# A decay-weighted attention and a gated feed-forward on one core: later copies of turned keys, weight words through a byte conversion, weight guards moved into the loop, and a new list of work

## The chip, the core and the metric

The kernel runs on one core of a Trainium2 chip. Its engines work side by side, each on its own queue of instructions: TensorE (PE), VectorE (DVE), ScalarE (ACT) and GpSimd (POOL); SyncE (SP) starts most transfers. The metric is the device time of one execution in microseconds, the median of the runs shown.

## What is computed

For each of 4 batches and 8 heads a 48x48 state runs over 768 tokens. Its output, 3072 rows of 384, goes through a gated feed-forward of width 1536. The weights come as float64.

```python
for t in range(S):
    kt, vt, rt, wt = (k[:, :, t], v[:, :, t], r[:, :, t], w[:, :, t])
    cur = np.einsum('bhd,bhe->bhde', u[None] * kt, vt)
    y[:, :, t] = np.einsum('bhd,bhde->bhe', rt, state + cur)
    state = wt[:, :, :, None] * state + np.einsum('bhd,bhe->bhde', kt, vt)
...
gate = 1.0 / (1.0 + np.exp(-(x @ w_gate)))
val = x @ w_val
return (gate * val @ w_out).astype(np.float32)
```

## The kernel before

Attention is cut into 24 chunks q of 128 tokens: batch q % 4, position q // 4. Four chunks of one position make a tile n of 512 rows for the feed-forward, and there are six tiles. The feed-forward's width is cut into 12 blocks f of 128; a block's weights (a third each for gate, value and output) are 128 x 1152 values.

For a chunk, `load_pin` and `load_tok` fetch decay, keys and queries, and values. VectorE scans the decay (`scan_k`, `prep_r`) and scales keys and queries. The keys are turned: early by TensorE (`turn_k`, then `take_k` copies them from its bank to `kT`); from chunk 10 on (`AWAY`) by VectorE, block by block, and by two transfers through device memory, `far_k` out and four reads `bk` back, after which ScalarE's three copies in `take_k` (L428, L430) make `kT`. TensorE computes scores and sums, VectorE masks (`mask`), TensorE applies (`states`, `mix`), ScalarE takes the result out (`take_y`), and it is turned into columns (`turn_x`, `take_x`, `rest_x`). The term of the current token goes through GpSimd (`bonus1`, `bonus2`, `bonus4`) and VectorE (`bonus3`). For the chunks in `LANES` (0, 1, 2) GpSimd multiplies queries by keys once (`in_lanes`), and TensorE sums with small matmuls (L421).

A float64 weight becomes a float32 word by bits. `w_body` and `w_sign` put the high word, shifted left by 3 and with its top bits kept, into a spare tile `temp`; `w_tail` joins the top 3 bits of the low word and writes over the low word. That is three VectorE passes. `w_guard` squares the high words on ScalarE and sums two tests, of which `check_bounds` makes a flag; if it is set, the slow path `general` runs behind everything. For tile 0, the blocks in `EXACT` (0 to 4) are multiplied as float32, in parts of 1 or 2 chunks (`SINGLE`, halves); the others are split into a high and a low part (`w_hi` on ScalarE, `w_lo` on VectorE) and take three matmuls where one stood.

The first stage holds chunks 0 to 7, all weights and tile 0. Its order comes from a planner (`Plan`). Each operation has an engine, a cost, what it waits for and a rank; the ranks come from the lists `TURNS` and `COMES` (the order of transfers on SP) and from the offsets in `LAGS` and `LATE`. `keep_busy` matmuls fill TensorE early on.

The loop then runs tiles 1 to 5, 12 steps each, in an order written by hand. A step issues `gate` and `sigmoid`, `value`, `hidden`, `hidden_hi` and `hidden_lo`, and `down` of the step before. It has four slots (0 to 3) in which other work is queued by `at(time, ...)`, where time counts slots from the loop's start. The visit to chunk q (`both`: states and outputs of q, scores and sums of q + 1) stands at a time that is 7 modulo 12. What prepares chunk q + 1 stands up to eight slots before. `take_k` of a key that goes through memory stands at `late`, time - 3, ahead of a step's sigmoid on ScalarE. In the first loop tile the `EXACT` blocks are split (`WHEN`). `leave` copies a finished tile out, on ScalarE and, for the last tile, on VectorE too.

In the rows below L638 and L641 are a step's matmuls for gate (`pg`) and value (`pu`), L681 those of `down` (`po`), L635 and L677 the exact ones, L651 the sigmoid, L658 `hidden`, L662 `hidden_hi`, L722 the fillers, L280 and L281 the guards, L285, L288 and L291 the words, L300 and L303 the split, L333, L336 and L340 the bonus products, L347 `in_lanes`.

## Time and profile before

| what | value |
|---|---|
| median of 3 runs | 560.25 us (557.87 to 560.35) |
| the profiled execution's own time | 565.31 us |
| its span, first to last instruction | 563.5 us |
| TensorE busy | 541.9 us (96%) |
| VectorE busy | 339.4 us (60%) |
| ScalarE busy | 218.9 us (39%) |
| GpSimd busy | 105.4 us (19%) |
| moved by DMA | 63.80 MB, mean 113 GB/s |

The busy shares are means over a first stage and a loop with different limits, so the rows below go by stretches. Matmuls are pipelined: the durations of single groups overlap, and the starts of the groups tell the pace.

### The profile page before, as it was taken

To read this page: it belongs to the slowest core of one execution; us is meant where nothing else is said; L and a number is where in the kernel's file an instruction comes from. 1 tells how busy PE (TensorE), PEld (TensorE's weight loads), DVE (VectorE), ACT (ScalarE), POOL (GpSimd) and SP (SyncE) were. 2 spreads that over 40 slices of the span, in tenths; PEclk is the share of its full clock that TensorE was granted. 3 is DMA by queue.
4 is the path that set the end of the run, shared out by engine and by line. 5 is a ranking of instruction groups with operands and counts; after the bars stand their busy time and mean duration, and the time that the engine had idled before them with its cause. 6 is when DMAs were issued, how large, how long until landed. Compare 5 with 4: busy or idle time off the path is not lost.

```text
span 563.5 us, 12729 instructions
## 1 busy us (share of the span) xinstructions
PE 541.9 (96%) x5395; PEld 448.0 (80%) x5395; DVE 339.4 (60%) x503; ACT 218.9 (39%) x428; POOL 105.4 (19%) x86
## 2 busy tenths in 40 slices
PE   8889899999999999999999999999999999999994
PEld 6777788877878888878888878887888888888883
DVE  5678998899677765656655656665655632321221
ACT  4568743743544334334234334234334322312211
POOL 5241503061103203203203303203203200000000
PEclk9698999999999999999999999999999999999998
DMA  8379502811343343243343343333343310100001
GB/s 325 139 263 422 202 0 100 303 64 30 128 126 111 94 145 116 97 128 105 98 145 101 113 130 106 94 103 136 119 124 112 95 31 1 56 2 0 1 0 62
DMA packets 30292, 63.80 MB, mean 113 GB/s; under 512 B 9617, under 2 KB 18706, under 8 KB 28690
## 3 DMA queue, kind: packets, MB, share of 16 engines
q1 hardware_dynamic: 28066, 58.97, 30.3%
q10 hardware_dynamic: 2160, 3.93, 1.8%
q8 instruction: 44, 0.72, 0.5%
q14 instruction: 22, 0.18, 0.1%
HBM read 52.14 MB, written 10.75 MB: 112 GB/s over the span
## 4 chain that ended last, share of the span: by engine, by line
PE 69%; DVE 10%; DMA 8%; ACT 5%; issue 2%; POOL 2%; SPq 1%; ACTq 0%; DVEq 0%
PE po L681 17%; PE pg L638 13%; PE pu L638 13%; PE pu L641 6%; PE pg L641 6%; DMA pin<-dec 3%; DVE sg L658 2%; DMA bk<-far_k 2%; PE po L677 2%; PE pa L457 2%; DMA raw<-wts 2%; DVE w L303 2%; PE py L477 2%; PE py L471 2%; PE pa L463 1%
## 5 line engine op out<-in xcount | busy, mean ns | idle before, releaser
L658 DVE TENSOR_TENSOR sg<-pu,sg 128x512 f32<-128x512 f32 (+2 forms) x78 | 50.6, 648 | 124.9 <-PE pu L641 104.7
L681 PE MATMUL po<-hh,w 128*128 128x512 f32 x402 | 124.8, 392 | 0.0
L638 PE MATMUL pg<-x,w 128*128 128x512 f32 x402 | 105.0, 396 | 0.0
L638 PE MATMUL pu<-x,w 128*128 128x512 f32 x402 | 102.5, 390 | 0.0
L651 ACT ACTIVATE sg<-pg 128x512 f32<-128x512 f32 (+2 forms) x78 | 44.1, 565 | 117.3 <-PE pg L641 87.5
L333 POOL TENSOR_TENSOR bon<-tok,ub 128x384 f32<-128x384 f32 x21 | 38.3, 1822 | 273.2 <-DVE x L626 180.9
L662 ACT CAST hh<-sg 128x512 fp32r<-128x512 f32 x67 | 41.5, 620 | 120.6 <-DVE sg L658 120.6
L638 PEld LDWEIGHTS pu<-x,w 128*128 128x128 f32 x402 | 75.2, 188 | 15.6
L681 PEld LDWEIGHTS po<-hh,w 128*128 128x128 f32 x402 | 74.9, 188 | 15.2
L638 PEld LDWEIGHTS pg<-x,w 128*128 128x128 f32 x402 | 73.7, 188 | 15.7
L681 PE MATMUL po<-hl,w 128*128 128x512 f32 x201 | 78.3, 390 | 0.2 <-DVE hl L666 0.2
L666 DVE TENSOR_TENSOR hl<-sg,hh 128x512 fp32r<-128x512 f32 x67 | 47.6, 711 | 41.7 <-ACT hh L662 41.7
L641 PE MATMUL pg<-x,w 128*128 128x512 f32 x201 | 56.6, 390 | 0.0
L641 PE MATMUL pu<-x,w 128*128 128x512 f32 x201 | 56.5, 389 | 0.0
L681 PEld LDWEIGHTS po<-hl,w 128*128 128x128 f32 x201 | 37.7, 188 | 8.7 <-DVE hl L666 0.8
L641 PEld LDWEIGHTS pg<-x,w 128*128 128x128 f32 x201 | 37.7, 188 | 8.0
L641 PEld LDWEIGHTS pu<-x,w 128*128 128x128 f32 x201 | 37.7, 188 | 7.9
L354 POOL TENSOR_TENSOR at<-eye,a 128x512 f32<-128x512 f32 x24 | 30.1, 1255 | 63.8 <-DVE a L340 55.7
L361 DVE TENSOR_TENSOR_SCAN eg<-pin,ends 112x516 f32<-112x516 f32 x24 | 30.7, 1278 | 8.3 <-DMA pin<-dec 5.7
L547 DVE COPY_PREDICATED at<-after,pa 128x512 f32<-128x512 int32 x24 | 17.7, 736 | 22.6 <-PE pa L463 20.1
L336 POOL TENSOR_TENSOR bon<-bon,tok 128x384 f32<-128x384 f32 x21 | 29.2, 1392 | 1.6
L381 DVE TENSOR_TENSOR_SCAN eg<-pin,heads 112x516 f32<-112x516 f32 x24 | 29.4, 1226 | 0.0
(101 smaller groups left out, 681.9 us busy)
## 6 DMA issues: line engine op xcount, KB each, us to landing
pin<-dec SPq DMA_DIRECT2D x23, 772.0 KB, 5.1
raw<-wts SPq DMA_DIRECT2D x12, 1152.0 KB, 10.1
tok<-tok SPq DMA_DIRECT2D x21, 576.0 KB, 4.3
y<-o ACTq DMA_DIRECT2D x15, 256.0 KB, 2.5
far_k<-bk SPq DMA_DIRECT2D x14, 256.0 KB, 2.0
bk<-far_k SPq DMA_DIRECT2D x56, 64.0 KB, 2.0
far_x<-bx SPq DMA_DIRECT2D x12, 192.0 KB, 3.2
bon<-far_x SPq DMA_DIRECT2D x48, 48.0 KB, 2.0
```

Of the source, the lines that this page charges most:

```text
L333: nc.gpsimd.tensor_tensor(out=bon[q], in0=tk[q][:, 0:DM], in1=ub, op=ALU.mult)
L336: nc.gpsimd.tensor_tensor(out=bon[q], in0=bon[q], in1=tk[q][:, DM:2 * DM], op=ALU.mult)
L354: engine.tensor_tensor(out=att[q], in0=eye.unsqueeze(1).unsqueeze(1).broadcast_to(shape), in1=a0, op=ALU.mult)
L361: nc.vector.tensor_tensor_scan(out=e[:, 516:0:-1], data0=t[:, 516:0:-1], data1=ends[:, 516:0:-1], initial=0.0, op0=ALU.mult, op1=ALU.add,)
L381: nc.vector.tensor_tensor_scan(out=e[:, WW:WW + 516], data0=t[:, 0:516], data1=heads[:, 0:516], initial=0.0, op0=ALU.mult, op1=ALU.add,)
L638: nc.tensor.matmul(t, lhsT=w[f][:, cols], rhs=x[n][:, a, k, spot], start=k == 0 and j == 0, stop=False)
L641: nc.tensor.matmul(t, lhsT=whi[f][:, cols], rhs=x[n][:, 1, k, i0 * C:i1 * C], start=False, stop=k == NKT - 1)
L651: nc.scalar.activation(sg, hid["g", n, f, i0], AF.Sigmoid)
L658: nc.vector.tensor_tensor(out=sg, in0=hid["u", n, f, i0], in1=sg, op=ALU.mult)
L662: nc.scalar.copy(hh, hid["s", n, f, i0])
L666: nc.vector.tensor_tensor(out=hl, in0=hid["s", n, f, i0], in1=hid["hi", n, f, i0].bitcast(F32), op=ALU.subtract)
L681: nc.tensor.matmul(to, lhsT=w[f][:, cols], rhs=h, start=first and i == 0, stop=last and i == 2, skip_group_check=True)
```

## The change

- `take_k` of keys that go through memory moves from `late` (time - 3) to time - 1.
- `w_body` and `temp` go. ScalarE reads the top byte of each low word, scales it by 1/32 and writes its integer part, the top 3 bits, over the low word (`top_bits`). VectorE joins the shifted high word (`w_sign`) and restores the top bits (`w_tail`), both in place.
- `w_guard` leaves the first stage. In the loop, from its second tile on and once in 12 slots, a block's float64 weights are fetched again into a buffer that is free by then (`again`), and three ScalarE passes test them (`w_square`, `w_small`, `w_large`). A small probe of the conversion's rounding joins the flag.
- The list: four exact blocks in place of five, three of them starting in quarters (`SINGLE`); no `LANES`; block 11 in two parts (`PAIRS`); new `TURNS`, `COMES`, `LAGS`, `LATE`; fillers stop once `po` exists.
- In the last tile the last part of `leave` is split in two, over ScalarE and VectorE and over two issuing engines.

```diff
-TURNS = "c0 w0 c1 c2 c3 w1 w2 w3 w4 w5 c4 w6 c5 w7 c6 w8 w9 w10 w11 c7"
-COMES = "ub p0 w0 p1 t0 w1 w2 t1 p2 t2 t3 w3 p3 w4 w5 w6 w7 t4 p4 w8 p5 t5 w9 p6 t6 p7 w10 w11 p8 t7 t8 t9 p9"
-SINGLE = [0]
-WIDE = [5, 6, 7, 8, 9, 10, 11]
-EXACT = [0, 1, 2, 3, 4]
+TURNS = "c0 w0 c1 c2 w1 c3 w2 w3 c4 c5 w4 w5 w6 w7 w8 c6 w9 w10 c7 w11"
+COMES = "ub p0 w0 t0 p1 w1 t1 t2 p2 w2 w3 p3 t3 t4 w4 t5 w5 p4 w6 p5 w7 p6 t6 w8 w9 w10 p7 t7 p8 t8 w11 p9 t9"
+SINGLE = [0, 1, 3]
+WIDE = [4, 5, 6, 7, 8, 9, 10, 11]
+EXACT = [0, 1, 2, 3]
...
-LAGS = [0, 11.5, -11.5, 103.0]
-LATE = dict(b3=-1.2, wl=-15.0, xl=17.5, wg=6.5, gd=51.5)
+LAGS = [0, -37.0, -28.5, 86.5]
+LATE = dict(b3=0.15, wl=1.0, xl=30.5, gd=72.5, wb=-2.0)
...
-PAIRS = []
-LANES = [0, 1, 2]
-RK = "POOL"
+PAIRS = [11]
+LANES = []
+RK = "DVE"
...
-    def w_guard(f):
-        sq = stage.tile([P, 3 * DM], BF16, tag="sq", name=f"sq{f}")
-        nc.scalar.activation(sq, word(f, 1, F32), AF.Square, accum_out=acc_s[:, f:f + 1])
-        nc.scalar.activation(sq, sq, AF.Relu, bias=1.0, scale=-1.0 / TINY ** 2, accum_out=acc_t[:, f:f + 1])
-
     def w_body(f):
-        t = temp[f] = stage.tile([P, 3 * DM], I32, tag="temp", name=f"temp{f}")
-        nc.vector.tensor_scalar(out=t, in0=word(f, 1), scalar1=3, scalar2=0x3FFFFFF8, op0=ALU.logical_shift_left, op1=ALU.bitwise_and)
+        top = raws[f].bitcast(U8).rearrange("a (c w) -> a c w", w=8)[:, :, 3]
+        top_bits(word(f, 0), top)
+
+    def top_bits(to, of):
+        nc.scalar.activation(to, of, AF.Copy, bias=-15.5 / 32, scale=1.0 / 32)
 
     def w_sign(f):
-        nc.vector.scalar_tensor_tensor(out=temp[f], in0=word(f, 1), scalar=-0x40000000, in1=temp[f], op0=ALU.bitwise_and, op1=ALU.bitwise_or)
+        nc.vector.scalar_tensor_tensor(out=word(f, 0), in0=word(f, 1), scalar=3, in1=word(f, 0), op0=ALU.logical_shift_left, op1=ALU.bitwise_or)
 
     def w_tail(f):
-        nc.vector.scalar_tensor_tensor(out=word(f, 0), in0=word(f, 0), scalar=29, in1=temp[f], op0=ALU.logical_shift_right, op1=ALU.bitwise_or)
+        nc.vector.scalar_tensor_tensor(out=word(f, 0), in0=word(f, 1), scalar=0x3FFFFFFF, in1=word(f, 0), op0=ALU.bitwise_or, op1=ALU.bitwise_and)
+
+    def again(f):
+        raws[f] = const.tile([P, 3 * DM], I64, tag=f"w{SPLITS[-1]}", name=f"again{f}")
+        nc.sync.dma_start(raws[f], wts[f])
+
+    def w_square(f):
+        nc.scalar.activation(word(f, 0, F32), word(f, 1, F32), AF.Square)
+
+    def w_small(f):
+        nc.scalar.activation(word(f, 1, F32), word(f, 0, F32), AF.Relu, bias=1.0, scale=-1.0 / TINY ** 2, accum_out=acc_t[:, f:f + 1])
+
+    def w_large(f):
+        nc.scalar.activation(word(f, 1, F32), word(f, 0, F32), AF.Relu, bias=most, scale=1.0, accum_out=acc_s[:, f:f + 1])
...
+            for cols in (slice(0, 2 * C), slice(2 * C, B * C)) if n == NC_ - 1 and j == NKT - 1 else (slice(0, B * C),):
...
     def keep_busy():
-        nc.tensor.matmul(lull[:, :P], lhsT=ident, rhs=ident, start=True, stop=True)
+        if not po:
+            nc.tensor.matmul(lull[:, :P], lhsT=ident, rhs=ident, start=True, stop=True)
...
-        add(f"wg{f}", "ACT", 2.85, [f"words{f}", f and f"wg{f - 1}"], k + LATE["wg"], w_guard, f)
-        add(f"wb{f}", "DVE", 0.83, [f"words{f}", f and f"wb{f - 1}"], k, w_body, f, take=["temp"])
+        add(f"wb{f}", "ACT", 1.2, [f"words{f}", f and f"wb{f - 1}"], k + LATE["wb"], w_body, f)
...
         if away_k(q):
-            at(late, take_k, q)
+            at(time - 1, take_k, q)
...
+    for f in range(NFF):
+        at(row + 12 * f + 5, again, f)
+        at(row + 12 * f + 9, w_square, f)
+        at(row + 12 * f + 13, w_small, f)
+        at(row + 12 * f + 14, w_large, f)
```

## Rows read from the trace of the kernel before

**Rows 1.** The page: TensorE's busy time in us, its share of the span and its instructions.

```profile
PE 541.9 (96%) x5395; PEld 448.0 (80%) x5395; DVE 339.4 (60%) x503; ACT 218.9 (39%) x428; POOL 105.4 (19%) x86
```

**Rows 2.** Busy time of each engine in four stretches of the first stage (start:end, length, busy us of each engine with its instructions, granted clock, DMA share, GB/s).

```profile
0.00:20.00 20.00, 15.54 (x212) 12.99 (x213) 12.70 (x15) 10.77 (x18) 8.79 (x20) 0.90 0.76 291
20.00:46.00 26.00, 23.25 (x406) 20.38 (x406) 18.66 (x27) 13.86 (x31) 8.87 (x6) 0.83 0.62 232
46.00:98.00 52.00, 49.96 (x569) 42.10 (x567) 47.38 (x62) 30.70 (x57) 14.93 (x9) 0.99 0.42 165
98.00:143.00 45.00, 44.78 (x588) 36.17 (x588) 40.35 (x51) 23.52 (x40) 11.33 (x7) 1.00 0.38 144
```

**Rows 3.** The same, for the filler matmuls of L722 alone (PE, PEld); the two later stretches have none.

```profile
0.00:20.00 20.00, 8.87 (x46) 7.90 (x47) 0.90 0.76 291
20.00:46.00 26.00, 3.91 (x16) 3.23 (x15) 0.83 0.62 232
```

**Rows 4.** The chain of work that ended last, in order of time, from the visit in the lap of 22.41 us to a step without a visit (start us, us, what).

```profile
241.57 0.25 PE pz L471
...
243.18 0.39 PE pa L463 x30
...
249.92 1.36 PE pg L638 x6
...
254.00 2.04 PE po L681 x9
```

**Rows 5.** Busy time of each engine in laps of the loop, each from the end of one visit to the end of the next (columns as in rows 2).

```profile
221.16:243.57 22.41, 21.27 (x214) 17.48 (x213) 12.73 (x20) 8.60 (x20) 3.94 (x3) 1.00 0.34 122
...
305.55:327.93 22.38, 21.24 (x213) 17.48 (x213) 12.73 (x20) 8.61 (x20) 4.23 (x3) 1.00 0.35 122
...
369.34:391.05 21.71, 20.84 (x195) 17.20 (x194) 12.99 (x21) 7.08 (x17) 4.26 (x3) 1.00 0.35 108
391.05:412.46 21.41, 21.20 (x197) 17.43 (x197) 11.89 (x18) 8.57 (x19) 3.41 (x3) 1.00 0.35 126
...
432.97:453.47 20.50, 20.50 (x194) 16.98 (x194) 12.20 (x19) 6.98 (x17) 4.27 (x3) 1.00 0.36 114
```

**Rows 6.** Who waited for whom over the whole span (us in total, times, longest us).

```profile
ACT kT L428 <- DMA bk<-far_k: 39.5, 13, 4.6
...
ACT sq L280 <- DMA raw<-wts: 11.6, 7, 3.1
```

**Rows 7.** ScalarE's instructions in order of time, in the lap of 22.41 us (start us, us; idle time before it and what ended that).

```profile
238.91 0.41 ACT L428 COPY kT<-bk 128x256 f32<-128x256 f32 x1 [2.92 <-DMA bk<-far_k]
...
240.20 0.60 ACT L651 ACTIVATE sg<-pg 128x512 f32<-128x512 f32 x1
```

**Rows 8.** VectorE's instructions in the same lap.

```profile
240.83 0.69 DVE L658 TENSOR_TENSOR sg<-pu,sg 128x512 f32<-128x512 f32 x1 [4.29 <-ACT sg L651]
```

**Rows 9.** Groups of instructions by line and shape over the whole span (count, busy us, mean ns of one, idle us before them and what ended it).

```profile
L333 POOL TENSOR_TENSOR bon<-tok,ub 128x384 f32<-128x384 f32 x21 | 38.3, 1822 | 273.2 <-DVE x L626 180.9 <-DMA tok<-tok 63.1 <-ACT kT L433 20.6
...
L336 POOL TENSOR_TENSOR bon<-bon,tok 128x384 f32<-128x384 f32 x21 | 29.2, 1392 | 1.6
...
L291 DVE SCALAR_TENSOR_TENSOR raw<-raw,temp 128x1152 int32<-128x1152 int32 x12 | 17.9, 1492 | 0.1
...
L303 DVE TENSOR_TENSOR w<-raw,w 128x1152 fp32r<-128x1152 f32 x12 | 16.6, 1380 | 0.9 <-ACT w L300 0.9
L280 ACT ACTIVATE sq<-raw 128x1152 bf16<-128x1152 f32 x12 | 15.2, 1270 | 11.6 <-DMA raw<-wts 11.6
...
L281 ACT ACTIVATE sq<-sq 128x1152 bf16<-128x1152 bf16 x12 | 14.0, 1164 | 0.4
...
L340 DVE TENSOR_REDUCE a<-bon 128x8 f32<-128x384 f32 x21 | 11.5, 549 | 10.0 <-POOL bon L336 10.0
...
L285 DVE TENSOR_SCALAR temp<-raw 128x1152 int32<-128x1152 int32 x12 | 10.4, 869 | 0.0
...
L347 POOL TENSOR_TENSOR bon<-pin 112x512 f32<-112x512 f32 x3 | 4.9, 1646 | 6.4 <-DMA pin<-dec 5.8 <-POOL at L354 0.6
...
L421 PE MATMUL pk<-weigh,bon 112*64 112x2 f32 x48 | 2.3, 216 | 0.0
```

**Rows 10.** The loads of weights (L273), from issue to landing.

```profile
DMA to landing us min/median/max: 6.5/10.1/17.6
```

**Rows 11.** The chain of work that ended last, in the first stage: half a block's exact groups.

```profile
71.09 1.29 PE pg L635 x6
72.39 1.46 PE po L677 x6
73.84 1.29 PE pu L635 x6
```

**Rows 12.** TensorE's instructions in order of time: the exact groups of one quarter (idle time before them in brackets, where there is any).

```profile
27.16 0.97 PE L635 MATMUL pg<-whole,raw 128*128 128x128 f32 x6
27.97 0.87 PE L635 MATMUL pu<-whole,raw 128*128 128x128 f32 x6
```

**Rows 13.** VectorE's instructions in order of time: a `w_tail` of the first block.

```profile
12.30 2.32 DVE L291 SCALAR_TENSOR_TENSOR raw<-raw,temp 128x1152 int32<-128x1152 int32 x1
```

**Rows 14.** GpSimd's instructions in order of time, at the same time.

```profile
11.00 2.40 POOL L347 TENSOR_TENSOR bon<-pin 112x512 f32<-112x512 f32 x1 [3.39 <-DMA pin<-dec]
```

**Rows 15.** ScalarE's instructions in order of time: the last copy.

```profile
556.08 0.59 ACT L689 COPY o<-po 128x512 f32<-128x512 f32 x1 [0.80 <-PE po L681]
```

More of the change, by code (lines that the diff above doesn't have):

```diff
@@ L13 @@
 I32 = mybir.dt.int32
+U8 = mybir.dt.uint8
 I64 = mybir.dt.int64
@@ L262, in tile_kernel @@
     nc.gpsimd.memset(ones, 1.0)
+    most = const.tile([P, 1], F32, name="most")
+    nc.gpsimd.memset(most, 2.0 ** -22 - 4.0)
     line = stage.tile([1, P + DM], F32, tag="sq", name="line")
@@ L265, in tile_kernel @@
     state = [const.tile([L, NP, D], F32, name=f"state{b}") for b in range(B)]
-    const.tile([P, 8], F32, name="spacer")
-    raws, temp, whi, wlo = {}, {}, [None] * NFF, [None] * NFF
+    raws, whi, wlo = {}, [None] * NFF, [None] * NFF
     def fetch(f):
@@ L685, in leave @@
         for j in range(NKT):
-            if n == NC_ - 1 and j == 1:
-                nc.vector.tensor_copy(o[:, j], po[n][j])
-            else:
-                nc.scalar.copy(o[:, j], po[n][j])
-            (nc.sync if n == NC_ - 1 else nc.scalar).dma_start(out[n, j * P:(j + 1) * P], o[:, j])
+            for cols in (slice(0, 2 * C), slice(2 * C, B * C)) if n == NC_ - 1 and j == NKT - 1 else (slice(0, B * C),):
+                late = cols.start > 0
+                if n == NC_ - 1 and j == 1 or late:
+                    nc.vector.tensor_copy(o[:, j, cols], po[n][j][:, cols])
+                else:
+                    nc.scalar.copy(o[:, j, cols], po[n][j][:, cols])
+                (nc.sync if n == NC_ - 1 and (late or j < NKT - 1) else nc.scalar).dma_start(out[n, j * P:(j + 1) * P, cols], o[:, j, cols])
     def check_bounds():
@@ L694, in check_bounds @@
         nc.vector.tensor_scalar(out=fine[:, 1], in0=acc_x, scalar1=0.0, scalar2=0.0, op0=ALU.mult, op1=ALU.is_equal)
-        nc.vector.tensor_scalar(out=fine[:, 2, :NFF], in0=acc_s, scalar1=1e10, scalar2=None, op0=ALU.is_le)
+        nc.vector.tensor_scalar(out=fine[:, 2, :NFF], in0=acc_s, scalar1=0.0, scalar2=None, op0=ALU.is_equal)
         nc.vector.tensor_scalar(out=fine[:, 3, :NFF], in0=acc_t, scalar1=0.0, scalar2=None, op0=ALU.is_equal)
+        probe, found = stage.tile([P, 8], U8, name="probe"), stage.tile([P, 8], I32, name="found")
+        nc.gpsimd.memset(probe, 32)
+        top_bits(found, probe)
+        nc.vector.tensor_scalar(out=fine[:, 3, NFF:NFF + 8], in0=found, scalar1=1.0, scalar2=None, op0=ALU.is_equal)
         p1.tile([P, 8], F32, name="margin")
@@ L772, in tile_kernel @@
         add(f"words{f}", "SP", 2.8, [], comes[f"w{f}"], fetch, f)
-        add(f"wg{f}", "ACT", 2.85, [f"words{f}", f and f"wg{f - 1}"], k + LATE["wg"], w_guard, f)
-        add(f"wb{f}", "DVE", 0.83, [f"words{f}", f and f"wb{f - 1}"], k, w_body, f, take=["temp"])
+        add(f"wb{f}", "ACT", 1.2, [f"words{f}", f and f"wb{f - 1}"], k + LATE["wb"], w_body, f)
         add(f"ws{f}", "DVE", 1.53, [f"wb{f}"], k, w_sign, f)
-        add(f"wt{f}", "DVE", 1.45, [f"ws{f}"], k, w_tail, f, give=["temp"])
+        add(f"wt{f}", "DVE", 1.45, [f"ws{f}"], k, w_tail, f)
         if f not in LATER:
@@ L779, in tile_kernel @@
             past = SPLITS[i - 1]
-            used = [f"wl{past}", f"wg{past}"] if i else []
+            used = [f"wl{past}"] if i else []
             add(f"wh{f}", "ACT", 1.26, [f"wt{f}"] + used, k + LATE["wl"], w_hi, f)
@@ L830, in at, with prepare @@
         todo.setdefault(time, []).append((f, a))
-    def prepare(q, early, turn, late, more):
+    def prepare(q, early, turn, late, more, time):
         at(early, bonus1, q)
@@ L864, in tile_kernel @@
         if q + 1 < NG:
-            prepare(q + 1, *EARLY[q - start] if q < start + B else (time - 8, time - 8, time - 3, time - 3))
+            prepare(q + 1, *EARLY[q - start] if q < start + B else (time - 8, time - 8, time - 3, time - 3), time)
         at(time, both, q)
```

2 lines of the change are left out of this document (1 added, 1 removed).

## The prediction

> **What bounds the kernel now.** I read the busy shares first: TensorE 96% [rows 1]. A busy TensorE can be waiting or filling, so I split the span. A first stage, ordered by the planner, ends at 143 us. A loop of 60 steps follows, with an attention "visit" about every third step, and a tail.
>
> In the first stage, TensorE's busy time less that of the `keep_busy` fillers is work that counts [rows 2, 3]: 133.53 - 12.78 = 120.8 us of 143. The 22.2 us that don't count lie at 0 to 20 us (13.3), at 20 to 46 (6.7), and hardly after that (2.0 and 0.2). From 46 us on TensorE's work sets the end. VectorE is close behind, busy 47.38 of 52 us and 40.35 of 45 [rows 2]; where TensorE's list gets shorter, VectorE's can take over.
>
> In the loop a step is 27 matmuls back to back: the groups `pg` and `pu`, 4.08 us from the first start (249.92) to that of `po` (254.00), and `po` of 2.04, 6.12 us in all [rows 4]. Between the ends of two visits lie three steps; the cheapest such lap is 20.50 us, with TensorE busy in all of it [rows 5]. Laps of 22.41, 22.38, 21.71 and 21.41 us stand over that floor by 1.91 + 1.88 + 1.21 + 0.91 = 5.9 us. The waits name a cause: ScalarE waits 39.5 us in 13 times for the keys that come back turned [rows 6]. Mostly that is free, but not in the long laps. In the lap of 22.41 the copies `kT` start at 238.91 us, when the keys land, and the sigmoid queued behind them starts at 240.20 [rows 7]. The product `sg` starts at 240.83, after 4.29 us of waiting for it [rows 8], and TensorE, which needs the product's bank `pu`, takes up the visit at 241.57 [rows 4].
>
> **The change part by part.** *Later key copies.* `take_k` moves from slot time-3, ahead of a sigmoid, to time-1, behind that step's `hidden_hi`. Its copies cost 1.3 us either way (238.91 to 240.20) [rows 7]. Undisturbed, product and `hidden_hi` are over some 1.4 us after the `pu` group, 0.6 before the `po` group ends; the copies would then end 0.7 us into the visit. They are needed by `sums`, which TensorE reached 1.6 us into it (243.18 against 241.57) [rows 4]. So the cover is about 0.9 us, and keys that land up to that much later still cost nothing. Behind the copies on ScalarE stand `guard` and `take_y`; the bank that `take_y` frees is wanted after the next `pg` group, 2.04 us. The move pays 0 to 5.9 us. I take 5.2, since each of the four laps may keep a tenth or two.
>
> *Weight guards in the loop.* Twelve times, from the second loop tile on, one reload of 1152 KB and three ScalarE passes. The guard's first pass took 1.27 us [rows 9]: 3.8 us a lap. ScalarE is busy for 7 to 8.6 us of a lap [rows 5], so there is room, and the passes stand where it waits for TensorE anyway, two behind a sigmoid and one behind `hidden_hi`. The reload adds two waits. On SP it waits for `w_large` of the weights before, with `load_pin`, the x transfers and `load_tok` queued behind it; that pass is over some 6 us into the lap, before these are due. On ScalarE `w_square` waits for the reload, with `hidden_hi` behind it. From the `hidden_hi` before `w_large` to the one behind `w_square` are two steps and a visit, 12.2 + 2.1 us; less one cast (0.6) and two passes (2.6) that leaves 11.1 us for the landing. Loads of this size landed in 6.5 us at best and 10.1 at the median, most with several in flight [rows 10]. I take 0.4 us for the whole; 0 if all lands in time, and the upper end is a rival.
>
> *Weight words.* Gone from VectorE: 12 passes of 0.87 us, 10.4. Two passes a block stay; they now read and write at 8-byte steps, as the one of 1.49 us did already [rows 9]. Gone from ScalarE in this stage: 12 x (1.27 + 1.16) us. New there: 12 byte conversions. No row shows one that reads bytes. The passes over the same 1152 columns took 1.16 and 1.27 us on ScalarE and up to 1.49 on VectorE [rows 9]; 1.16 and 1.49 are the ends, and I take 1.27, the pass with the same steps on the same engine. ScalarE gets about 14 us lighter. But the conversion waits for its words at the head of ScalarE's queue, with the attention's copies and sigmoids behind it. The guards waited 11.6 us in 7 times [rows 6], and the conversion stands earlier in the list than they did.
>
> *New list.* One block of weights fewer goes through exact matmuls. An exact half takes 1.29 + 1.46 + 1.29 us [rows 11], a block 8.1, a split block 6.12: -2.0 us of TensorE. Without `LANES` 48 small matmuls go, -2.3 us [rows 9], in the part with gaps. Two more blocks start in quarters: a quarter's group took 0.81 us from start to start [rows 12] against 1.29 for a half, so 2 x 3 x (2 x 0.81 - 1.29) = +2.0 us, which can start earlier and fill gaps. Net -2.3 us of TensorE. VectorE: -10.4, +1.4 for one more `w_lo`, +1.6 for three more `bonus3` [rows 9], -7.4 us. GpSimd: three products of 1.65 us become three pairs of 1.82 + 1.39 [rows 9], +4.7 us. The token loads of three chunks grow from 192 to 576 KB. The ends for the stage are wide. With TensorE's gaps as they are, -2.3. If VectorE sets the pace at its share of now (119.1 of 143 [rows 2]), -7.4 / 0.83 = -8.9. With a list that fits worse, 0 or above. From 46 us on TensorE has no gaps, so I stay near the first end: -2.3, and a third of the 6.7 us between 20 and 46, -2.2: -4.5.
>
> GpSimd's extra work speaks against that. A `w_tail` took 2.32 us beside a GpSimd product of 2.40 [rows 13, 14], against the mean of 1.49 [rows 9]. The Trainium skill ("SBUF — State Buffer", Who interferes with whom) says that VectorE and GpSimd share one port pair under an exclusive lock, and the loser waits for the whole instruction. The trace agrees as far as that pass goes. By that rule all of GpSimd's added 4.7 us could land on VectorE, and the stage would gain nothing.
>
> *Tail.* The last copy of 0.59 us [rows 15] is split over two engines, and its transfer with it: -0.4 us (0 to -0.6). The probe of the conversion's rounding is three tiny operations, hidden under a step's matmuls; uncovered it would cost under 1 us.
>
> **Sum.** -5.2 + 0.4 - 4.5 - 0.4 = -9.7 us. The profiled execution took 565.31 us (span 563.5 and 1.8 around it), so it would take 555.6. The median of the runs shown is 5.1 us lower, 560.25, so I forecast 550.5 us.
>
> **The rivals.** (A) *The first stage does not get shorter*: VectorE, held up by GpSimd's longer products, eats the 4.5 us. For it: VectorE's 91% from 46 to 98 us. Against: 7.4 us less work there. 555.0 us.
>
> (B) *The keys still come late*: the reload starts right behind the key reads and slows them by more than the cover of 0.9 us. For it: loads of one size landed between 6.5 and 17.6 us [rows 10], depending on what else moved. The Trainium skill ("DMA: Bandwidth & Descriptors", Issuing engines are not separate DMA queues) says that all transfers run on the same 16 engines and interleave; the row agrees. Against: the reads are issued first, and in the long laps the DMA engines are only 34 to 35% busy [rows 5]. 555.7 us.
>
> (C) *Slower: conversions hold ScalarE.* The words land later than the list assumes, ScalarE stands at each of the 12 conversions, and the copies behind it reach TensorE late. For it: the guards' 11.6 us of waits. Against: a guard that waited held nothing up from 98 us on, where TensorE had no gap. If each conversion waits as a guard did on average (1.66 us) and TensorE stands for all of it, +19.9 us: 570. It takes back the whole gain from 0.8 us each on.
>
> (D) *The reload becomes the wait*: each us of landing beyond 11.1, and some 2 us more until TensorE wants the result, costs up to 1 us on each of 12 laps. At the slowest landing, 17.6 us, 12 x 4.5 = 54: 604. Against: nothing else of this size moves in the loop.
>
> (E) *No change*: A and B together, 560. (F) *It doesn't do what it says*: if the conversion rounds otherwise than assumed, the probe raises the flag and the path `general` runs behind everything, far longer than the kernel itself; the trace doesn't show it.
>
> **How the numbers follow.** Forecast 0.63 (546 to 554), A 0.16, B 0.09, C 0.06, D 0.02, E 0.03, F 0.01. The forecast's low end is the full 5.9 us of the loop with 8.9 in the first stage and 0.6 in the tail, 545. Upward the range takes in A and B with their spread, to 558, so 545 to 558; C to F, 0.12, lie outside with a little of the others. A measurement of this kernel tells about 0.5% from no change, here 2.8 us, so faster means under 557.4. Forecast, A and nearly all of B give 0.85; E with edges of A and B 0.07; C, D and F with the edge of E 0.08.
>
> **What would show it.** Laps near 20.5 us throughout, no sigmoid behind `kT`. The first copy of `leave` at about 138.5 us in place of 143. Conversions near 1.27 us. No wait of ScalarE for reloads. I am wrong if laps with a reload stay above 21 us (B, D), or if TensorE shows gaps after 46 us (A, C).

## The result and the profile after

The changed kernel took 564.48 us, the median of 17 runs (561.21 to 566.53); the kernel before, run beside it, 560.29 (557.15 to 564.95, 17 runs). The ratio is 1.0072, 95% interval 1.0050 to 1.0093: slower by 0.7%, where the forecast was 1.7% faster. The profiled execution of after took 566.53 us, its span 564.0. Disturbed runs are left out of every comparison here, which puts three medians a little under those that the expectations below name (556.66 us for 556.9, 554.97 for 555.3, 561.98 for 562.5).

The busy shares, which answer [rows 1], hardly differ; the whole line shows what moved, ScalarE from 218.9 to 246.0 us:

```profile
PE 540.5 (96%) x5401; PEld 447.2 (79%) x5401; DVE 337.4 (60%) x500; ACT 246.0 (44%) x454; POOL 109.1 (19%) x91
```

The first stage in the same four stretches as [rows 2] (busy us of each engine with its instructions, granted clock, DMA share, GB/s):

```profile
0.00:20.00 20.00, 14.03 (x166) 11.97 (x170) 12.50 (x14) 6.47 (x9) 11.17 (x23) 0.98 0.67 257
20.00:46.00 26.00, 24.08 (x519) 21.26 (x508) 24.19 (x31) 15.29 (x32) 13.96 (x9) 0.95 0.69 268
46.00:98.00 52.00, 48.55 (x597) 40.65 (x596) 42.55 (x55) 25.42 (x39) 11.17 (x8) 0.93 0.61 233
98.00:143.00 45.00, 44.72 (x522) 36.97 (x521) 39.82 (x54) 18.90 (x33) 13.27 (x9) 1.00 0.26 92
```

From 46 to 98 us TensorE is now busy 48.55 of 52 us at a clock of 0.93, where it had 49.96 at 0.99 [rows 2]: 3.5 us of gaps where there were 2.0, and a lower clock behind the longest of them. The first copy of `leave`, which marks the stage's end, starts at 141.15 us; before it was at 143.02, in an execution 5 us above its own median. Such a mark varies from one profile to the next. Five of the profiles have the first stage of after unchanged (after and four experiments below: the old end, one slot later, no guards, reloads alone), and in them it lies between 136.8 and 141.2 us; the old stage has it at 143.0 in the kernel before and at 137.3 in late keys alone. So the profiles show no shorter stage, one of them says little, and the stage's worth is taken from medians.

The loop varies less. From that first copy of `leave` to the last matmul the kernel before took 413.0 us and after 413.7.

The loop's laps (columns as above), cut from visit to visit as in [rows 5]: one without a reload, then two with one.

```profile
178.04:198.57 20.53, 20.53 (x212) 17.02 (x210) 14.20 (x22) 8.41 (x17) 4.26 (x3) 1.00 0.35 113
...
261.34:282.62 21.28, 21.08 (x212) 17.32 (x210) 13.10 (x21) 10.53 (x21) 4.26 (x3) 1.00 0.51 165
282.62:303.92 21.30, 21.10 (x212) 17.32 (x210) 13.11 (x21) 10.52 (x21) 4.26 (x3) 1.00 0.51 165
```

The laps of 22.4 us [rows 5] are gone. In their place eight laps of 21.27 to 21.30 us stand between 240 and 452 us: all that hold a reload and no `leave`. The two with both take 20.95 and 20.90.

The groups that answer [rows 9] (count, busy us, mean ns of one, idle us before them and what ended it), conversion, `w_sign`, `w_tail`, the three guard passes and the first key copy:

```profile
L291 DVE SCALAR_TENSOR_TENSOR raw<-raw 128x1152 int32<-128x1152 int32 x12 | 17.3, 1444 | 0.0
L288 DVE SCALAR_TENSOR_TENSOR raw<-raw 128x1152 int32<-128x1152 int32 x12 | 16.2, 1351 | 4.3 <-ACT raw L285 4.3
L304 ACT ACTIVATE again<-again,most 128x1152 f32<-128x1152 f32 x12 | 16.1, 1340 | 0.0
...
L285 ACT ACTIVATE raw<-raw 128x1152 int32<-128x1152 uint8 x12 | 15.4, 1286 | 16.0 <-DMA raw<-wts 16.0
...
L298 ACT ACTIVATE again<-again 128x1152 f32<-128x1152 f32 x12 | 14.8, 1237 | 0.0
L301 ACT ACTIVATE again<-again 128x1152 f32<-128x1152 f32 x12 | 14.8, 1232 | 0.0
...
L441 ACT COPY kT<-bk 128x256 f32<-128x256 f32 x14 | 5.6, 401 | 0.0
```

The last line answers [rows 6]: the key copies no longer wait for their keys. The guard passes wait for nothing (0.0), so no reload is late. The reloads, from issue to landing (count, KB each, median us), against 10.1 us for the first loads [rows 10]:

```profile
again<-wts SPq DMA_DIRECT2D x12, 1152.0 KB, 5.4
```

One wait is new, VectorE's for ScalarE's `take_x` (us in total, times, longest):

```profile
DVE x L639 <- ACT x L626: 11.3, 10, 1.5
```

I followed it through the lap of 21.30 us. ScalarE, then VectorE, then GpSimd, in order of time (start us, us; in brackets the idle time before and what ended it):

```profile
294.49 1.34 ACT L304 ACTIVATE again<-again,most 128x1152 f32<-128x1152 f32 x1
...
295.81 0.51 ACT L626 ACTIVATE x<-bon 128x384 fp32r<-128x384 f32 x1
...
301.60 0.62 ACT L675 CAST hh<-sg 128x512 fp32r<-128x512 f32 x1 [3.75 <-DVE sg L671]
302.12 0.40 ACT L441 COPY kT<-bk 128x256 f32<-128x256 f32 x1
302.55 0.83 ACT L443 COPY kT<-bk 64x256 f32<-64x256 f32 x2
```

```profile
296.45 0.56 DVE L639 TENSOR_TENSOR x<-bon,x 128x384 fp32r<-128x384 f32 x1 [1.14 <-ACT x L626]
...
300.41 0.55 DVE L353 TENSOR_REDUCE a<-bon 128x8 f32<-128x384 f32 x1 [0.91 <-POOL bon L349]
300.88 0.68 DVE L671 TENSOR_TENSOR sg<-pu,sg 128x512 f32<-128x512 f32 x1
```

```profile
297.09 1.87 POOL L346 TENSOR_TENSOR bon<-tok,ub 128x384 f32<-128x384 f32 x1 [16.23 <-DVE x L639]
299.04 1.34 POOL L349 TENSOR_TENSOR bon<-bon,tok 128x384 f32<-128x384 f32 x1
```

The chain reads downwards. `w_large` (L304) stands ahead of `take_x` (which begins at L626) on ScalarE and ends when that begins. `rest_x` (L639) on VectorE has waited 1.14 us for it; `bonus1` and `bonus2` on GpSimd wait for `rest_x`, whose buffer they reuse; `bonus3` (L353) waits for them; and behind it in VectorE's queue stands the product of the next step (L671), then `hidden_hi` (L675), and behind that the key copies that this change moved there. They end at 303.38 us. TensorE reaches `sums` at 303.06:

```profile
303.06 0.93 PE L476 MATMUL pa<-tok,kT 64*48 64x48 f32 x32
```

### The profile page after: what moved, and what is told of

It reads as the page before. It is cut to its first block, busy times and chain, and to the rows that moved or that the text cites. A ratio compares the mean times of both kernels' runs of the same rounds, so it can differ in the third digit from the quotient of the medians.

```text
span 564.0 us, 12788 instructions
## 1 busy us (share of the span) xinstructions
PE 540.5 (96%) x5401; PEld 447.2 (79%) x5401; DVE 337.4 (60%) x500; ACT 246.0 (44%) x454; POOL 109.1 (19%) x91
## 4 chain that ended last, share of the span: by engine, by line
PE 65%; DVE 10%; ACT 6%; DMA 6%; POOL 5%; issue 4%; SPq 1%; ACTq 0%; DVEq 0%
PE po L694 16%; PE pg L651 13%; PE pu L651 13%; PE pu L654 6%; PE pg L654 6%; DMA raw<-wts 4%; POOL bon L346 3%; DVE sg L671 3%; POOL bon L349 2%; PE pa L476 2%; PE po L690 2%; ACT kT L443 1%; PE py L490 1%; DMA far_k<-bk 1%; PE py L484 1%
## 5 line engine op out<-in xcount | busy, mean ns | idle before, releaser
L694 PE MATMUL po<-hh,w 128*128 128x512 f32 (+1 forms) x414 | 127.0, 388 | 0.0
L671 DVE TENSOR_TENSOR sg<-pu,sg 128x512 f32<-128x512 f32 (+2 forms) x80 | 50.8, 635 | 109.6 <-PE pu L654 97.9
L651 PE MATMUL pg<-x,w 128*128 128x512 f32 (+1 forms) x414 | 107.0, 394 | 0.0
L651 PE MATMUL pu<-x,w 128*128 128x512 f32 (+1 forms) x414 | 104.5, 388 | 0.0
L675 ACT CAST hh<-sg 128x512 fp32r<-128x512 f32 (+1 forms) x69 | 42.3, 613 | 117.5 <-DVE sg L671 117.5
L651 PEld LDWEIGHTS pu<-x,w 128*128 128x128 f32 x414 | 76.7, 188 | 15.6
L651 PEld LDWEIGHTS pg<-x,w 128*128 128x128 f32 x414 | 75.3, 188 | 15.5
L694 PE MATMUL po<-hl,w 128*128 128x512 f32 (+1 forms) x207 | 80.2, 387 | 0.1
L679 DVE TENSOR_TENSOR hl<-sg,hh 128x512 fp32r<-128x512 f32 (+1 forms) x69 | 48.2, 699 | 42.9 <-ACT hh L675 42.9
L654 PE MATMUL pg<-x,w 128*128 128x512 f32 (+1 forms) x207 | 57.7, 387 | 0.0
L654 PE MATMUL pu<-x,w 128*128 128x512 f32 (+1 forms) x207 | 57.6, 386 | 0.0
L367 POOL TENSOR_TENSOR at<-eye,a 128x512 f32<-128x512 f32 x24 | 32.3, 1345 | 68.6 <-DVE a L353 68.6
L654 PEld LDWEIGHTS pg<-x,w 128*128 128x128 f32 x207 | 38.6, 188 | 8.1
L654 PEld LDWEIGHTS pu<-x,w 128*128 128x128 f32 x207 | 38.6, 188 | 7.9
L349 POOL TENSOR_TENSOR bon<-bon,tok 128x384 f32<-128x384 f32 x24 | 34.9, 1455 | 1.9
L560 DVE COPY_PREDICATED at<-after,pa 128x512 f32<-128x512 int32 x24 | 17.7, 739 | 22.0 <-PE pa L476 19.8
```

Source lines behind the costliest of these rows:

```text
L349: nc.gpsimd.tensor_tensor(out=bon[q], in0=bon[q], in1=tk[q][:, DM:2 * DM], op=ALU.mult)
L367: engine.tensor_tensor(out=att[q], in0=eye.unsqueeze(1).unsqueeze(1).broadcast_to(shape), in1=a0, op=ALU.mult)
L651: nc.tensor.matmul(t, lhsT=w[f][:, cols], rhs=x[n][:, a, k, spot], start=k == 0 and j == 0, stop=False)
L654: nc.tensor.matmul(t, lhsT=whi[f][:, cols], rhs=x[n][:, 1, k, i0 * C:i1 * C], start=False, stop=k == NKT - 1)
L671: nc.vector.tensor_tensor(out=sg, in0=hid["u", n, f, i0], in1=sg, op=ALU.mult)
L675: nc.scalar.copy(hh, hid["s", n, f, i0])
```

## The experiments

Medians are each of 5 to 12 runs, the kernel before beside them at 560.7 to 561.0 us. A ratio's interval is 0.2 to 0.4% to either side, so differences of 1 to 2 us between two experiments are at the edge of what they tell.

**One slot later.** My theory was the chain above. The edit puts `w_large` behind `take_x`:

```diff
-        at(row + 12 * f + 14, w_large, f)
+        at(row + 12 * f + (14 if f % B == B - 1 else 15), w_large, f)
```

> The changed kernel with w_large one slot later, behind take_x, in the eight laps where take_x stands in that slot (where leave stands there, it stays). First theory: w_large ahead of take_x makes take_x, rest_x, GpSimd's bonus1 and bonus2, then bonus3 and behind it the product of hidden late, and that costs each of the eight laps with a reload 0.75 us (21.28 against 20.53 in the laps without one). Then these laps fall to 20.5 us and the time from 564.5 to 558.5 us. Second theory: the reload itself, as a transfer beside the others, makes the laps longer; then they stay at 21.28 and the time at 564.5. Third theory: the key copies, now behind hidden_hi, keep the sums waiting; then nothing changes here either.

558.24 us, ratio 0.9954 [0.9933, 0.9975]: 6.2 us less than after. The same lap, from the visit before, with its ScalarE and VectorE rows and `sums`:

```profile
276.79:297.32 20.53, 20.53 (x214) 17.02 (x209) 12.89 (x21) 10.55 (x22) 4.26 (x3) 1.00 0.53 171
```

```profile
288.64 0.52 ACT L626 ACTIVATE x<-bon 128x384 fp32r<-128x384 f32 x1
...
289.16 1.35 ACT L304 ACTIVATE again<-again,most 128x1152 f32<-128x1152 f32 x1
```

```profile
289.38 0.55 DVE L639 TENSOR_TENSOR x<-bon,x 128x384 fp32r<-128x384 f32 x1
```

```profile
296.82 0.57 PE L476 MATMUL pa<-tok,kT 64*48 64x48 f32 x32
```

`rest_x` waits for nothing, and `sums` takes 0.57 us in place of 0.93. All eight laps fall to between 20.52 and 20.59 us; together they take 5.9 us less, and the stretch from the first copy of `leave` to the last matmul falls from 413.7 to 407.9 us. The same passes, the same ScalarE load, the same reloads, another order: the theory holds.

**No guards.** Reloads and passes left out, so the weights aren't tested for size; the two sums that the test reads are set to zero.

```diff
-    for f in range(NFF):
-        at(row + 12 * f + 5, again, f)
-        at(row + 12 * f + 9, w_square, f)
-        at(row + 12 * f + 13, w_small, f)
-        at(row + 12 * f + 14, w_large, f)
+    nc.gpsimd.memset(acc_s, 0.0)
+    nc.gpsimd.memset(acc_t, 0.0)
```

> The changed kernel without the reloads and the three passes of the weight guards; the sums of the guards are set to zero once, so the test of the weights is left out. First and second theory: the laps fall to 20.5 us, 558.5 us or a little under. Third theory (key copies): the laps stay near 21.28 and the time near 564. If the first theory is right, this and the run with w_large moved come out within 0.5 us of each other.

556.66 us, ratio 0.9922 [0.9897, 0.9947]. The guards in the loop cost 7.8 us in after, 1.6 of it still there when they stand well. In the loop itself nothing of it is left then: from the first copy of `leave` to the last matmul this kernel takes 407.8 us, and 407.9 with the guards one slot later.

**The old end.** After with the last copy and its transfer whole again.

```diff
-            for cols in (slice(0, 2 * C), slice(2 * C, B * C)) if n == NC_ - 1 and j == NKT - 1 else (slice(0, B * C),):
...
+            if n == NC_ - 1 and j == 1:
+                nc.vector.tensor_copy(o[:, j], po[n][j])
+            else:
+                nc.scalar.copy(o[:, j], po[n][j])
+            (nc.sync if n == NC_ - 1 else nc.scalar).dma_start(out[n, j * P:(j + 1) * P], o[:, j])
```

> The changed kernel with the last tile's copies and transfers as before (three whole parts). The profiled execution of the changed kernel ended 9.1 us after its last matmul group, the one before 7.4 us. If the split of the last part causes that, the tail is 7.4 us again and the time 563 us, about 1.5 less; if the end of a program varies by that much anyway, the time stays within 0.5 us of 564.5, or rises by the 0.4 us that the split was meant to give.

564.17 us, ratio 1.0066 [1.0043, 1.0089], against 564.48 with the split. The split changes nothing that can be measured, and without it the program still ends 8.8 us behind its last matmul.

**Late keys alone.** The kernel before with `take_k` moved, and nothing else.

```diff
-            at(late, take_k, q)
+            at(time - 1, take_k, q)
```

> The kernel before with the key copies two slots later and nothing else. If the long laps of the profiled execution (21.4 to 22.4 us) stand in most executions, the laps fall to 20.5 to 20.9 and the time from 560.3 by some 4 to 5 us to 556. If they were peculiar to the one profiled execution, whose time was 5 us over the median, the time stays at 560.3, and the laps that were 20.5 stay so. If the later copies keep the sums waiting, those laps rise.

554.97 us, ratio 0.9921 [0.9894, 0.9947]: 5.7 us by the medians, 4.4 by the ratio, and 4.2 from the first copy of `leave` to the last matmul (408.8 us). The laps that answer the two of 22.4 us [rows 5], and ScalarE at the end of the first of them, answering [rows 7]:

```profile
216.15:237.08 20.93, 20.93 (x217) 17.30 (x213) 13.10 (x20) 8.78 (x21) 3.88 (x3) 1.00 0.38 131
...
298.73:319.67 20.94, 20.94 (x218) 17.31 (x213) 12.73 (x20) 8.43 (x19) 4.37 (x3) 1.00 0.37 130
```

```profile
231.74 0.60 ACT L651 ACTIVATE sg<-pg 128x512 f32<-128x512 f32 x1 [0.47 <-DVE pin L386]
234.00 0.62 ACT L662 CAST hh<-sg 128x512 fp32r<-128x512 f32 x1 [1.66 <-DVE sg L658]
234.52 0.40 ACT L428 COPY kT<-bk 128x256 f32<-128x256 f32 x1
```

The sigmoid no longer stands behind the copies, and they wait for nothing. This one line of the change makes the kernel before faster by more than its measurement is uncertain.

**Two edits of the new list.** In after TensorE has a gap of 3.0 us near 60 us (1.85 with `w_large` later). ScalarE, then TensorE, in after:

```profile
57.96 1.25 ACT L285 ACTIVATE raw<-raw 128x1152 int32<-128x1152 uint8 x1 [2.84 <-DMA raw<-wts]
...
62.56 1.31 ACT L285 ACTIVATE raw<-raw 128x1152 int32<-128x1152 uint8 x1 [3.08 <-DMA raw<-wts]
```

```profile
61.00 2.93 PE L690 MATMUL po<-sg,raw 128*128 128x256 f32 x6 [3.00 <-DVE sg L671]
```

The conversion stands at the head of ScalarE's queue and waits for its words, as rival C had it, with a sigmoid behind it; the load was queued on SP behind `load_tok` of chunk 5. So I swapped the two, with `w_large` later:

```diff
-... w3 p3 t3 t4 w4 t5 w5 p4 ...
+... w3 p3 t3 t4 w4 w5 t5 p4 ...
```

> The run with w_large moved (558.2 us), and in COMES the weights of block 5 ahead of the tokens of chunk 5. In three profiles of the new list ScalarE stands 3 to 3.6 us at a byte conversion that waits for its weights, with a sigmoid behind it, and TensorE idles 3.0 to 3.7 us near 60 us; SP had held that load back behind a token load that waited for a buffer. If that wait is what the new list loses, the gap near 60 us goes and the time falls by some 3 us to 555. If TensorE's work after 60 us or VectorE sets the end anyway, or the planner's order only moves the wait elsewhere, it stays within 1 us of 558.2.

580.13 us, ratio 1.0333 [1.0296, 1.0370]. Both expectations fail: TensorE now stands still for 6.8 and 10.7 us at 79 to 101 us. The list is what the planner orders every queue by, and with two entries swapped it laid out the whole stage another way.

The second edit is at the granted clock, with `w_large` later: ten more fillers on TensorE ahead of the turning of chunk 1's keys.

```diff
+        for _ in range(10 if q == 1 else 0):
+            keep_busy()
```

> The run with w_large moved, and ten more filler matmuls ahead of the turning of chunk 1's keys, where TensorE stood idle from 14.4 to 17.6 us. All four profiles with the new list show a granted clock of 0.5 to 0.66 in the stretch 20 to 24 us, the run with the old list and late keys shows 1.00 throughout. If that drop costs time, the fillers keep the clock at 1.00 and the time falls by 2 to 4 us, to 555. If TensorE waits for others in this stretch whatever its clock, the clock rises and the time stays within 0.7 us of 558.2. If the fillers hold up the keys, it rises.

556.81 us, ratio 0.9912 [0.9877, 0.9947], 1.4 us less than without. With the fillers TensorE is busy for all of 12 to 16 us, where it was for 2.75. The stretches from 16 to 24 us, without and then with the fillers:

```profile
16.00:20.00 4.00, 2.43 (x39) 2.15 (x43) 3.93 (x6) 0.62 (x2) 3.08 (x3) 0.74 0.01 3
20.00:24.00 4.00, 4.00 (x110) 3.55 (x105) 4.00 (x4) 2.12 (x5) 1.64 (x2) 0.50 0.44 159
```

```profile
16.00:20.00 4.00, 2.57 (x45) 2.23 (x47) 3.97 (x5) 1.58 (x2) 3.92 (x3) 1.00 0.03 10
20.00:24.00 4.00, 4.00 (x143) 3.51 (x136) 3.96 (x5) 2.69 (x7) 1.64 (x2) 1.00 0.58 166
```

The clock stays at 1.00, and TensorE does 143 instructions in place of 110 in the same 4 us. What that is worth to the whole, 1.4 us, lies inside the two intervals.

**The lanes.** With `w_large` later, the three chunks of the old list in lanes again.

```diff
-LANES = []
-RK = "DVE"
+LANES = [0, 1, 2]
+RK = "POOL"
```

> The run with w_large moved, with chunks 0 to 2 back in LANES (small matmuls in place of GpSimd's two products and VectorE's reduction, token loads of 192 KB). If GpSimd's longer work and the longer token loads at the start hold up the first chunks, TensorE's gap near 15 us shrinks, the clock stays higher near 20 us, and the time falls by 1 to 3 us. If not, it stays within 0.7 us of 558.2, or rises with the small matmuls' 2.3 us.

555.09 us, ratio 0.9889 [0.9856, 0.9923], 3.2 us less than without. With the late keys alone it is the fastest of the study that leaves nothing out. TensorE is then busy for all of 16 to 20 us (at a clock of 0.57), where it was for 2.43. The edit changes the products, VectorE's reductions and the token loads together, and which of them pays isn't separated.

Fillers and lanes together:

> The kernel with w_large one slot later and both gains of the first stage together: LANES [0, 1, 2] with RK on POOL (alone 3.2 us less), and ten more fillers before the turning of chunk 1's keys (alone 1.4 us less). Theory: the two are separate, the one being GpSimd's products and the other the granted clock at 16 to 24 us, so they add: 553.7 us, with the clock at 1.00 from 12 to 24 us. Rival: both shorten the same wait for chunk 1's attention, and the second adds nothing: 555 us.

556.59 us, ratio 0.9928 [0.9903, 0.9953]. They don't add, and the fillers bring nothing here; with the lanes TensorE's gap lies elsewhere, and the clock still fell to 0.63 at 16 to 20 us. The lanes gain 3.2 us without the fillers (558.24 to 555.09) and 0.2 with them (556.81 to 556.59), and 555 us is no firmer than that.

**Old and new list, old and new words.** With `w_large` later throughout, the guards in the loop and the keys late. First the old `TURNS`, `COMES`, `SINGLE`, `WIDE`, `EXACT`, `LAGS`, `PAIRS`, `LANES` and `RK`, with the new words:

```diff
-TURNS = "c0 w0 c1 c2 w1 c3 w2 w3 c4 c5 w4 w5 w6 w7 w8 c6 w9 w10 c7 w11"
-EXACT = [0, 1, 2, 3]
-LATE = dict(b3=0.15, wl=1.0, xl=30.5, gd=72.5, wb=-2.0)
+TURNS = "c0 w0 c1 c2 c3 w1 w2 w3 w4 w5 c4 w6 c5 w7 c6 w8 w9 w10 w11 c7"
+EXACT = [0, 1, 2, 3, 4]
+LATE = dict(b3=-1.2, wl=-15.0, xl=17.5, gd=51.5, wb=0.0)
...
```

> The run with w_large moved, with the list of before (TURNS, COMES, SINGLE, EXACT, LAGS, PAIRS, LANES) in place of the new one; the byte conversion takes the rank of the old first pass. If the new list is what loses in the first stage, against 10.4 us less of VectorE's work, the time falls by 3 us or more, to 555 or less. If the conversion on ScalarE loses it under any list, the time stays at 558, with ScalarE standing for weights here too. If the new list is the better one, it rises to 560.

579.25 us, ratio 1.0296 [1.0255, 1.0337]. TensorE's wait and the group behind it, and the stretch around it:

```profile
104.82 0.98 PE L429 MATMUL pk<-ident,pin 112*128 112x112 f32 x4 [14.98 <-issue]
105.47 2.91 PE L651 MATMUL pg<-x,w 128*128 128x512 f32 x6
```

```profile
88.00:104.00 16.00, 1.57 (x6) 1.10 (x6) 14.98 (x15) 7.34 (x6) 0.00 (x0) 0.65 0.14 59
```

TensorE is busy for 1.57 of 16 us, VectorE for 14.98. The exact groups are used up, the first split group (L651) starts at 105.47, and between them VectorE works off ten passes over weights of 1.35 us each, ahead of the step (`prep_k`) that the next chunk's keys wait for. I took it to be the conversion that the old list doesn't fit. So I put the old words back too, as in the kernel before (L285, L288 and L291 there), with the guards still in the loop:

```diff
-        top = raws[f].bitcast(U8).rearrange("a (c w) -> a c w", w=8)[:, :, 3]
-        top_bits(word(f, 0), top)
+        t = temp[f] = stage.tile([P, 3 * DM], I32, tag="temp", name=f"temp{f}")
+        nc.vector.tensor_scalar(out=t, in0=word(f, 1), scalar1=3, scalar2=0x3FFFFFF8, op0=ALU.logical_shift_left, op1=ALU.bitwise_and)
...
-        add(f"wb{f}", "ACT", 1.2, [f"words{f}", f and f"wb{f - 1}"], k + LATE["wb"], w_body, f)
+        add(f"wb{f}", "DVE", 0.83, [f"words{f}", f and f"wb{f - 1}"], k, w_body, f, take=["temp"])
```

> The old list with the old three VectorE passes for the words, but the weight guards out of the first stage and in the loop, w_large one slot later, keys copied late. The old list with the new words took 579.3 us, with a hole of some 14 us in TensorE's work at 90 to 105. Theory: it is the conversion on ScalarE that the old list doesn't fit, so with the old words the hole is gone: 554 to 557 us, the 555.3 of the late keys alone, plus 1.3 for the longer end, less up to 3 for ScalarE's 29 us of guards that left the stage. Rival: any change of what the planner has to place opens such a hole, the removal of the guards too: 570 or more.

575.66 us, ratio 1.0266 [1.0228, 1.0305]. The theory falls: the hole is there without any conversion (a wait of 7.3 us, and the first split group at 97.74). In the first stage this kernel differs from late keys alone only by the guards that are gone, 2.85 us a block in the plan, and by three fillers less: that was enough to make the old list a bad one. The fourth corner, the old words under the new list, by the same edit:

> The new list with the old words: the three VectorE passes in place of the byte conversion and two passes, all else as in the kernel with w_large one slot later (558.2 us). It completes a square: old list with old words, guards out of the first stage, 575.7; old list with new words 579.3; new list with new words 558.2. Theory: with the guards out of the stage, what the list is decides, and the words are worth little by themselves: VectorE gets 12 passes of 0.76 to 0.87 us back, 9 to 10 us, and ScalarE loses 15.4; 558 to 563. Rival: the list fits only the operations it was made for, whichever are changed; then a hole of 7 us or more opens between the last exact group and the first split group here too, 567 or more.

561.98 us, ratio 1.0038 [1.0010, 1.0066]. No hole opens: from 20 us on TensorE's longest wait is 2.6 us. Side by side, all with the guards out of the first stage:

| | old words | new words |
|---|---|---|
| old list | 575.7 | 579.3 |
| new list | 562.0 | 558.2 |

The new words cost 3.6 us under the old list and save 3.7 under the new one. The list saves 14 us with the old words and 21 with the new. Neither has a worth of its own.

**What is left of the guards.** The reloads without the passes (the weights untested again), with `w_large` gone as well:

```diff
-        at(row + 12 * f + 9, w_square, f)
-        at(row + 12 * f + 13, w_small, f)
-        at(row + 12 * f + (14 if f % B == B - 1 else 15), w_large, f)
+    nc.gpsimd.memset(acc_s, 0.0)
+    nc.gpsimd.memset(acc_t, 0.0)
```

> The kernel with w_large one slot later, but with only the twelve reloads in the loop: the three ScalarE passes on each are left out, so the weight guards test nothing. With passes the median was 558.2 us, without passes and reloads 556.9. Theory: the laps cost the same in all three, and the 1.3 us stand behind the last matmul, where the kernels with guards in the loop end 8.8 to 9.6 us after it and those without 6.7 to 7.4; if the twelve reloads on SP's queue make that end longer, this kernel takes 558 us and ends about 9 us after its last matmul. Rival: the passes do it; then it takes 557 and ends about 7.3 us after.

555.09 us, ratio 0.9899 [0.9857, 0.9940]: the theory about the reloads falls, they cost nothing. Behind the last matmul after ends 9.1 us later, this kernel 7.6. What the instruction fetches of one queue were (packets, MB, share of 16 engines), first after:

```profile
q14 instruction: 23, 0.19, 0.1%
```

and with the reloads alone:

```profile
q14 instruction: 22, 0.18, 0.1%
```

Every profile with the passes in the loop (ten) has 23 or 24 such packets and ends 8.8 to 9.6 us behind its last matmul; every one without them (four, the kernel before among them) has 22 and ends after 6.7 to 7.6.

## Why the prediction was wrong

| Term | forecast, us | by medians, us | by ratios (x 560), us | from |
|---|---|---|---|---|
| later key copies | -5.2 | -5.7 | -4.4 | late keys alone less before |
| weight guards in the loop | +0.4 | +7.8 | +8.4 | after less no guards |
| list and words, split end | -4.9 | +1.7 | +0.1 | no guards less late keys |
| sum | -9.7 | +3.8 | +4.0 | after less before |

**Later key copies: right** in mechanism, and in size within what was measured, 4.4 to 5.7 us. The floor was set a little low: the four long laps fell by 4.5 us together, to 20.93, 20.94, 20.67 and 20.91, and not to 20.50. Three of them hold a `leave`, and a lap with one takes 20.9 us in the experiments too.

**Guards in the loop: the step that failed.** I wrote that "ScalarE is busy for 7 to 8.6 us of a lap [rows 5], so there is room, and the passes stand where it waits for TensorE anyway". The busy share was right (10.5 us now, of 21), and the two waits I named were harmless: the reloads landed in 5.4 us at the median and 9.3 at most where I allowed 11.1, and rivals B and D, which hung on them, fall with that. The laps with a reload did stay above 21 us, my sign for B or D, but by neither of the two. What I left out is who stands *behind* a pass on ScalarE. I named `hidden_hi` for `w_square` and nobody for `w_large`; it was `take_x`, and through VectorE and GpSimd the next step's product. Three passes of 1.2 to 1.3 us cost 0.74 us in each of eight laps, 5.9 us in the profiles and 6.2 by the medians, shown by moving one of them by one slot. The rest, 1.6 us, fits the later end of the program (7.3 us behind the last matmul without guards, 9.6 with the guards one slot later).

The two halves of the change also meet here. The key copies were moved behind `hidden_hi`, and by my own sum that left a cover of 0.9 us; the late product used that up. By the rows, the product starts 1.2 us later against TensorE's visit than with `w_large` behind `take_x` (300.88 with the visit at 301.22, against 293.81 with it at 295.38). That the guards would have cost less with the keys copied early is argued from this; it wasn't tried.

**List and words: no gain where 4.5 us was forecast.** The prices of single passes came out close. A conversion took 1.286 us where I took 1.27 as the row with the same steps; VectorE's two passes 1.35 and 1.44 against 1.49. The sums over an engine did not. VectorE was to lose 7.4 us; up to the first copy of `leave` it is busy 117.3 us, against 119.1 before. TensorE's work that counts is 118.4 us (131.4 busy in the four stretches, less 11.1 of fillers, less the 1.9 that lie behind the stage's end) against 120.8, but part of that is the lower clock in the profile of the kernel before (0.83 from 20 to 46 us): late keys alone, with the same stage at 1.00, has 117.3, and the other four profiles with the stage of after 116.0 to 116.5. So the gain is about 1 us where -2.3 was worked out.

What failed most is the step behind the sums, "With TensorE's gaps as they are, -2.3 ... and a third of the 6.7 us between 20 and 46": gaps are not a reserve that less work runs into. One opened at 58 to 61 us behind a conversion that waited for its words. That is rival C, at 3 us in place of 20: ScalarE stood at conversions for 16.0 us in 8 times, and from 46 us on this is TensorE's only long wait. Another, at 14 to 18 us, got longer: 3.75 us, where the kernel before stood for 2.43 at that place. VectorE's rows there in after, then GpSimd's and TensorE's:

```profile
14.94 0.55 DVE L353 TENSOR_REDUCE a<-bon 128x8 f32<-128x384 f32 x1 [0.62 <-POOL bon L349]
...
16.76 1.26 DVE L383 TENSOR_TENSOR pin<-pin,eg 112x512 f32<-112x512 f32 x1
17.94 0.73 DVE L560 COPY_PREDICATED at<-after,pa 128x512 f32<-128x512 int32 x1
```

```profile
15.57 1.90 POOL L367 TENSOR_TENSOR at<-eye,a 128x512 f32<-128x512 f32 x1 [0.66 <-DVE a L353]
```

```profile
18.12 0.57 PE L429 MATMUL pk<-ident,pin 112*128 112x112 f32 x4 [3.75 <-issue]
...
18.86 0.77 PE L484 MATMUL py<-mid,pin 48*64 48x48 f32 x16
```

Without `LANES` the current token's term of chunk 0 goes through GpSimd's two products, VectorE (`bonus3`, L353), GpSimd again (`bonus4`, L367) and VectorE (`mask`, L560) before TensorE goes on with the chunk (L484), at 18.86 us; that was at 16.66 in the kernel before, and it is at 15.35 with the lanes back. Chunk 1's keys, which TensorE turns meanwhile (L429), are hardly earlier: their scaling (`prep_k`, L383) takes 1.26 us beside `bonus4`, an undisturbed one 0.68. Dropping `LANES`, which I booked as 2.3 us of TensorE saved, cost 3.2 us with `w_large` later (0.2 with the fillers too).

The square of four corners shows the error behind it: I added up the worth of the words, the guards' leaving and the list as if each had one. Under the old list, the same kernel with less work for ScalarE, and as much for VectorE, is 15 us slower than the kernel before. The new list is no improvement to be priced; it is what keeps the other edits from costing 20 us.

Of the port between VectorE and GpSimd I gave the row that spoke against the change [rows 13, 14]. After has it again in the first block: a `w_tail` of 2.04 us, with a GpSimd product of 1.99 beside it.

```profile
12.01 2.04 DVE L291 SCALAR_TENSOR_TENSOR raw<-raw 128x1152 int32<-128x1152 int32 x1
```

```profile
12.91 1.99 POOL L349 TENSOR_TENSOR bon<-bon,tok 128x384 f32<-128x384 f32 x1
```

An undisturbed pass takes 1.35 us, so the means of 1.351 and 1.444 hold 1.1 us of this in all 24 passes, less than the 4.1 us in the three old passes (1.35, 1.35 and 0.75 undisturbed). The Trainium skill ("SBUF — State Buffer", Who interferes with whom) says that a VectorE instruction with two inputs in SBUF contends with a GpSimd instruction that reads there; this row agrees with it. The delay moved to other passes: in the first stage of after ten scans and scalings of VectorE, all beside a GpSimd product, took 6.0 us more than undisturbed ones (1.23 and 0.69 us); late keys alone has two, 1.0 us, and the kernel before none. This speaks for rival A: the stage did not get shorter, and these 6.0 us took back half of the 12.0 that the words gave VectorE (45.5 us before, 33.5 in after). How much of the 4.5 us that accounts for isn't shown, since no run changes GpSimd's work alone.

**Split end.** Forecast -0.4, measured +0.3 of the median (564.48 with the split, 564.17 without), which can't be told from nothing. VectorE's half waits 0.4 us for ScalarE's half of the same bank, so the halves were copied one behind the other.

**The sum.** The measured rows are the steps from before to late keys alone, from there to no guards and from there to after, so they add up to the whole by construction (4.2 us by the result's own medians) and don't test each other. What tests the first two is the stretch from the first copy of `leave` to the last matmul: -4.2 us from before to late keys alone, and +5.9 from no guards to after, all but 0.1 of it gone one slot later. What is open is why the old list with the guards gone lays VectorE's passes over weights ahead of a chunk's keys, and whether the later end of the program is a fetch of instructions or something that comes with it.

## What to carry over

When an operation is put into an idle slot of an engine, list what stands behind it in that engine's queue and follow it to the engine that sets the end; the busy share of the lap says nothing about it, and one slot was worth 6 us here. When an order was made by a planner from a list, don't price the operations and the list apart: measure the corners, old list with new operations among them. And try each independent edit alone on the kernel before; the one line that moves the key copies is as fast, 555.0 us, as the best of all the rest with it, 555.1.
